# The wo load moved two value places up in the stream of a decode attention kernel, and its products moved behind its landing

## The chip, the cores and the metric

The kernel runs on one core of one Trainium2 chip. The metric is the device time of one execution in microseconds (us), taken from runs without the profiler; shown is the median of three. One more execution was taken with the profiler, and all views of the profile are of that one.

## The reference

One token is decoded. A gate mixes an attention block over a long key and value cache with a small gated MLP:

```python
def _A_ref(x, k_cache, v_cache, wq, wo):      # H = 32 heads, 65536 cached rows, Dh = 128, D = 512
    q = (x @ wq).reshape(B, Sq, H, Dh).transpose(0, 2, 1, 3)
    scores = jnp.einsum("bhqd,bhkd->bhqk", q, k_cache) * (Dh ** -0.5)
    p = _softmax(scores, axis=-1)
    o = jnp.einsum("bhqk,bhkd->bhqd", p, v_cache)
    return o.transpose(0, 2, 1, 3).reshape(B, Sq, H * Dh) @ wo
...
g = _sigmoid((x * gate_w).sum(-1, keepdims=True))
b = (silu(x @ w_gate) * (x @ w_up)) @ w_down  # F = 1792
return g * a + (1 - g) * b
```

All arrays are bf16. The keys and values of each head are 16 MiB each, so the two caches hold 1 GiB. The weight wo is 4096 x 512, 4 MiB.

## The kernel before, in words

**The stream.** Keys and values come through a ring of four slots of 4 MiB (`ring`, `NPL = 4`). A slot's filling is called a place: a quarter of one head's keys or of its values, 128 partitions by 128 cache rows. `plan_stream` writes the order of the places by hand: first wq, the MLP's weights and the keys of heads 0 and 1; then, for head h from 2 to 31, key places of head h alternating with value places of head h - 2; at last the eight value places of heads 30 and 31. The list `dmas` follows that order, and SyncE (SP) issues its entries one after another (L172 to L191). Ahead of each entry SP waits until the slot's former owner is used up: a key place by VectorE's transposes (`ktdone`), a value place by TensorE's products (`pvdone`). All waits and issues are on one queue, so an entry that waits holds back all that follow. The last value place of head 31 is issued in four parts that end at rows 64, 96, 112 and 128 (`ENDS`).

**wo.** It doesn't go through the ring. It is written into `kt`, the buffer of the transposed keys, which is free once the last scores have been computed; SP therefore waits for `qkdone` at `UN * H` (L187) before it issues wo. In `dmas` it stands behind the last value place of head 30, written ("v", H - 2, PL - 1) (L84). It has 32 x 128 rows of 1 KB; a place has 128 rows of 32 KB.

**Keys.** VectorE transposes half a place at a time (a unit, L334) from the ring to `kt`, and TensorE multiplies 16 times per unit into `psS` (L406). After a head's eight units come the maximum, the exponential on ScalarE and a transpose to `pb`.

**Values.** `values(h, t)` (L416) takes one place: 32 products of four cache rows each into row tile `psO` (L427), behind a wait for the landing. In place 1 of each head `turn` (L437) follows for the head before: eight small products that turn its finished row (`orow`, which ScalarE copied from `psO`) to a column in `psT`; ScalarE copies it to `oTn` (L234). The last place of all, ("v", H - 1, PL - 1), has another form: ahead of it `turn(H - 1)` brings what places 0 to 2 of head 31 gave to `psT` (ScalarE's copy for it is L262), and then 128 small products, row by row, are added there (L432).

**The output projection.** `project(h)` (L445) is one TensorE product of head h's column `oTn` with its 128 rows of wo, 1 x 512, added up in `psY` over all heads. It waits for ScalarE's copy of that column (`s_oc`), for the last head for VectorE's (`s_otn`). Behind `project(H - 1)` VectorE mixes in the MLP's row (L353), and ScalarE's queue stores the result.

**TensorE's order** at the end is the loop over `last` (L473 to L483): the places of heads 30 and 31 in turn; behind place 0 of head 31 a wait for wo's landing and `project` of heads 0 to 29; behind its place 1 (and the turn of head 30) `project` of head 30; then place 2, the turn of head 31, place 3 and `project` of head 31.

In the profile's lines an issue by SP is `SPq ... L191`, a value place is `psO ... L427 x32`, a product with wo is `psY ... L450`, a turn is `psT ... L441`, and the last place `psT ... L432 x128`.

## Time and profile before

| what | before |
|---|---|
| median of three runs | 2542.88 us (2542.84 to 2543.08) |
| profiled execution | 2542.47 us |
| its span, first to last instruction | 2540.6 us |
| mean granted TensorE clock | 0.914 |
| TensorE busy | 2046.1 us (81%) |
| VectorE busy | 1169.2 us (46%) |
| ScalarE busy | 56.8 us (2%) |
| key places on SP's queue | 128 of 4096 KB, 30.0 us from issue to landing (median) |
| whole value places on SP's queue | 127 of 4096 KB, 28.0 us (median) |
| wq, the first transfer of all | 4096 KB, 13.1 us |

The span is what the profile shows, and 1.87 us of the profiled execution's time lie around it. Busy shares are means over the whole span. The time from an issue to its landing holds the time that the transfers ahead of it on the queue still took. The chain of waits is followed back from the last instruction: at each step to what released it, or to the instruction before it on the same engine. An idle time in brackets at the end of a row is that of the engine just ahead of it, with what ended it.

### The profile page before, as it was taken

How to read it: one execution, taken by the hardware profiler on the slowest of the kernel's cores; microseconds unless marked ns; L12 is line 12 of the kernel's file. 1: busy time of each engine (PE TensorE's matmuls, PEld its weight loads, DVE VectorE, ACT ScalarE, POOL GpSimd, SP SyncE). 2: the span in 40 equal slices, each digit the busy share in tenths (PEclk: the TensorE clock that was granted, in tenths of full speed). 3: DMA queues.
4: the chain of work that ended last, by engine and by line, in shares of the span. 5: the costliest groups of instructions: out<-in, count | busy, mean ns of one | idle time of the engine just before them, and what ended most of it. 6: DMA issues, size and time to landing. Idle time of an engine off the chain costs nothing. (4 is left out here: it accounts for less than half of the span.)

```text
span 2540.6 us, 19360 instructions
## 1 busy us (share of the span) xinstructions
PE 2046.1 (81%) x8734; PEld 819.6 (32%) x8846; DVE 1169.2 (46%) x374; ACT 56.8 (2%) x194; POOL 26.1 (1%) x75
## 2 busy tenths in 40 slices
PE   5787788788878887888888888888887888788886
PEld 3333333333333333333333333333333333333333
DVE  4844544454454445444544444445445444444420
ACT  0000000000000000000000000000000000000000
POOL 0000000000000000000000000000000000000000
PEclk9989988998899889989899889998899888998898
DMA  9999999999999999999999999999999999999997
GB/s 414 431 432 430 432 431 433 431 431 434 430 431 433 432 430 433 431 430 432 434 430 431 434 431 431 434 430 431 433 432 430 434 431 430 433 432 431 432 425 317
DMA packets 42012, 1087.93 MB, mean 428 GB/s; under 512 B 4227, under 2 KB 8326, under 8 KB 8582
## 3 DMA queue, kind: packets, MB, share of 16 engines
q1 hardware_dynamic: 41988, 1087.65, 99.7%
q8 instruction: 11, 0.18, 0.0%
q14 instruction: 11, 0.09, 0.0%
q10 hardware_dynamic: 2, 0.00, 0.0%
HBM read 1087.64 MB, written 0.00 MB: 428 GB/s over the span
## 5 line engine op out<-in xcount | busy, mean ns | idle before, releaser
L334 DVE STREAM_TRANSPOSE kt<-ring 128x4096 uint32<-128x4096 uint32 x256 | 1125.7, 4426 | 1246.6 <-DMA ring<-in_A_k_cache_dram 1246.2
L406 PE MATMUL psS<-kt,qw 128*128 128x512 bf16 x3984 | 1095.7, 438 | 455.6 <-DVE kt L334 455.0
L427 PE MATMUL psO<-ring,pb 128*4 128x512 bf16 x4064 | 902.2, 380 | 19.4 <-DMA ring<-in_A_v_cache_dram 19.4
L406 PEld LDWEIGHTS psS<-kt,qw 128*128 128x128 bf16 x4096 | 425.7, 107 | 1111.3 <-DVE kt L334 420.8
L427 PEld LDWEIGHTS psO<-ring,pb 128*4 128x4 bf16 x4064 | 344.5, 87 | 568.8 <-issue 73.9
L246 ACT ACTIVATE nbias<-amx 128x1 f32<-128x1 f32 x32 | 6.5, 203 | 2348.6 <-POOL amx L212 2348.6
L350 DVE TENSOR_SCALAR oTn<-psT,Li 128x1 bf16<-128x1 f32 x1 | 0.2, 220 | 85.9 <-PE psT L432 85.9
L441 PEld LDWEIGHTS psT<-unit,orow 4*128 4x128 f32 x264 | 31.8, 186 | 15.1 <-issue 13.9
L212 POOL PARTITION_ALL_REDUCE amx<-mxs x32 | 11.3, 353 | 2369.1 <-DVE mxs L313 2369.1
L441 PE MATMUL psT<-unit,orow 4*128 4x1 f32 x264 | 34.6, 248 | 0.7 <-ACT orow L262 0.7
L319 DVE STREAM_TRANSPOSE pb<-pa 128x512 bf16<-128x512 bf16 x32 | 21.5, 671 | 6.4 <-PE psO L427 6.4
L313 DVE TENSOR_REDUCE mxs<-psS 128x1 f32<-128x512 f32 x32 | 20.9, 653 | 3.9 <-PE psS L406 3.9
L250 ACT ACTIVATE pa<-psS,nbias 128x512 bf16<-128x512 f32 x32 | 22.0, 687 | 2.6
L230 ACT ACTIVATE orow<-psO,Li 4x512 f32<-4x512 f32 x31 | 20.9, 675 | 21.6 <-PE psO L427 21.6
L214 POOL PARTITION_ALL_REDUCE Lt<-rsum x32 | 12.3, 385 | 38.0 <-ACT pa L250 38.0
L362 PE MATMUL psM<-ones,xrow 1*128 1x1 bf16 x4 | 0.3, 172 | 14.0 <-DMA gwrow<-in_gate_w_dram 14.0
L450 PE MATMUL psY<-kt,oTn 128*1 128x512 bf16 x32 | 7.6, 385 | 0.7 <-DVE oTn L350 0.4
L224 ACT COPY qw<-qd 128x16 bf16<-128x16 bf16 x32 | 7.9, 250 | 6.7 <-DVE qd L295 6.7
L383 PEld LDWEIGHTS psM<-xTb,ring 128*128 128x128 bf16 x112 | 6.9, 160 | 0.2
L383 PE MATMUL psM<-xTb,ring 128*128 128x1 bf16 x112 | 6.8, 198 | 0.0
L280 DVE CUSTOM_DVE_ANT_0 orow<-xrow,gwrow 1x512 f32<-1x512 bf16 x1 | 0.8, 837 | 12.0 <-DMA gwrow<-in_gate_w_dram 12.0
L234 ACT CAST oTn<-psT 128x1 bf16<-128x1 f32 x31 | 5.0, 162 | 55.6 <-PE psT L441 55.6
(41 smaller groups left out, 42.6 us busy)
## 6 DMA issues: line engine op xcount, KB each, us to landing
ring<-in_A_k_cache_dram SPq DMA_DIRECT2D x128, 4096.0 KB, 30.0
ring<-in_A_v_cache_dram SPq DMA_DIRECT2D x127, 4096.0 KB, 28.0
ring<-in_A_wq_dram SPq DMA_DIRECT2D x1, 4096.0 KB, 13.1
kt<-in_A_wo_dram SPq DMA_DIRECT2D x1, 4096.0 KB, 40.0
ring<-in_A_v_cache_dram SPq DMA_DIRECT2D x1, 2048.0 KB, 38.3
ring<-in_B_w_gate_dram SPq DMA_DIRECT2D x1, 1792.0 KB, 26.3
ring<-in_B_w_up_dram SPq DMA_DIRECT2D x1, 1792.0 KB, 30.0
ring<-in_B_w_down_dram SPq DMA_DIRECT2D x1, 1792.0 KB, 33.8
```

Source lines behind the costliest of these rows:

```text
L212: nc.gpsimd.partition_all_reduce(amx[:, h:h + 1], mxs[:, h:h + 1], P, RMAX).then_inc(s_ar, 1)
L214: nc.gpsimd.partition_all_reduce(Lt[:, h:h + 1], rsum[:, h:h + 1], P, RADD).then_inc(s_L, 1)
L224: nc.scalar.copy(qcol[:, h % 2], qd[:, h, :, :]).then_inc(s_qw, STEP)
L230: nc.scalar.mul(orow[0:4, :], psO[0:4, h % 2, :], Li[0:4, h:h + 1]).then_inc(s_or, STEP)
L250: nc.scalar.activation(pa[:, h % 2, :], psS[:, h % 2, :], ACT.Exp, bias=nbias[:, h:h + 1], scale=SCALE, accum_out=rsum[:, h:h + 1]).then_i ...
L313: nc.vector.reduce_max(mxs[:, h:h + 1], psS[:, h % 2, :], AX_X).then_inc(s_mx, 1)
L319: nc.vector.transpose(pb[:, h % 2, :], pa[:, h % 2, :]).then_inc(s_pb, STEP)
L334: nc.vector.transpose(o, src).then_inc(ktdone, 1)
L383: done = nc.tensor.matmul(psM[:, o + j:o + j + 1], w[:, c, :, j], xTb[:, c:c + 1], start=(c == 0), stop=(c == Dc - 1))
L406: done = nc.tensor.matmul(psS[:, h % 2, :], qw[:, h % 2, je, at0:at0 + 128], ktb[i % 2][:, je // 2, k, :, je % 2], start=(u == 0 and k == ...
L427: done = nc.tensor.matmul(psO[0:4, h % 2, :], pbk[:, h % 2, k, rho:rho + 4], v[:, r * Dh:(r + 4) * Dh], start=(t == 0 and r == 0), stop=(t ...
L441: done = nc.tensor.matmul(psT[:, h % 2:h % 2 + 1], orow[0:4, i * Dh:(i + 1) * Dh], unit[0:4, i:i + 1], start=(i == 0), stop=(i == 3 and h ...
```

## The change

wo's entry in `dmas` moves from behind place 3 of head 30 to behind its place 1, ahead of places 2 and 3. On TensorE the wait for wo's landing stands behind place 1 of head 30 and the turn that follows it; there the products of heads 0 to 28 are made. The product of head 29 stands behind place 2 of head 30. The product of head 30 moves from behind place 1 of head 31 to behind its place 2, ahead of the turn of head 31. The wait for `qkdone` ahead of wo's issue goes with the entry. The number of instructions on every engine is the same, and the order on VectorE, ScalarE and GpSimd is too.

```diff
@@ -81,7 +81,7 @@
-        if item == ("v", H - 2, PL - 1):
+        if item == ("v", H - 2, 1):
             landed["wo"] = len(dmas)
             dmas.append((("wo",), 0, 0, None, None))
@@ -474,11 +474,13 @@
                 if item == ("v", H - 1, PL - 1):
                     turn(H - 1)
                 run(item)
-                if item == ("v", H - 1, 0):
+                if item == ("v", H - 2, 1):
                     arrived(pe, landed["wo"])
-                    for h in range(H - 2):
+                    for h in range(H - 3):
                         project(h)
-                if item == ("v", H - 1, 1):
+                if item == ("v", H - 2, 2):
+                    project(H - 3)
+                if item == ("v", H - 1, 2):
                     project(H - 2)
             project(H - 1)
```

## The prediction

> I write V(h,t) for place t of head h's values; the last two heads are 30 and 31. All times are microseconds of the profiled execution's span unless said otherwise.

> **What bounds the kernel now.** First the page's DMA lines.

> ```profile
> q1 hardware_dynamic: 41988, 1087.65, 99.7%
> HBM read 1087.64 MB, written 0.00 MB: 428 GB/s over the span
> ```

> The 16 DMA engines are taken for 99.7% of the span, so the length is set by bytes. The change moves no byte in or out; it can only gain or lose where the last bytes have landed and work still follows, or by letting the queue run dry. So I read the end next, in the chain of waits over the last 45 us.

> ```profile
> 2457.57 43.09 DMA ring<-in_A_v_cache_dram
> ...
> 2500.80 9.41 PE psO L427 x32
> 2510.21 6.47 PE psY L450 x30
> 2516.68 6.91 PE psO L427 x32
> ...
> 2525.25 6.92 PE psO L427 x32
> ...
> 2533.92 3.35 PE psT L432 x128
> ```

> The reader is to see a DMA first, then an unbroken row of TensorE work: V(31,0), the 30 products with wo, V(31,1), V(31,2), V(31,3). From 2500.66 on, nothing waits for a landing. Is TensorE late against the stream there? The issues on SyncE's queue and their times to landing, read in narrow windows, answer it (timeline row: start, duration; issue row: size, us to landing).

> ```profile
> 2450.96 0.43 SPq L191 DMA_DIRECT2D kt<-in_A_wo_dram  x1
> kt<-in_A_wo_dram SPq DMA_DIRECT2D x1, 4096.0 KB, 40.0
> 2457.57 28.02 SPq L191 DMA_DIRECT2D ring<-in_A_v_cache_dram  x1
> ring<-in_A_v_cache_dram SPq DMA_DIRECT2D x1, 4096.0 KB, 43.1
> 2486.12 0.43 SPq L191 DMA_DIRECT2D ring<-in_A_v_cache_dram  x1
> ring<-in_A_v_cache_dram SPq DMA_DIRECT2D x1, 4096.0 KB, 34.0
> ```

> Start plus time to landing: wo at 2490.96, V(31,0) at 2500.67, V(31,2) at 2486.12 + 34.0 = 2520.1. The chain starts V(31,2) at 2525.25: TensorE is 5.1 late. V(31,3)'s last piece lands at 2488.16 + 41.8 = 2530.0, and its products run to 2533.92 + 3.35 = 2537.27. The lag was made at V(31,0): landed at 2500.66, it took 9.41, and the 30 products another 6.47, while the next place landed 9.7 later.

> Two other places are rows I need for prices, and three windows give TensorE's busy time and, after POOL's column, its granted clock.

> ```profile
> 2460.10 8.76 PE L427 MATMUL psO<-ring,pb 128*4 128x512 bf16 x32 [2.55 <-DMA ring<-in_A_v_cache_dram]
> ...
> 2479.61 7.07 PE L427 MATMUL psO<-ring,pb 128*4 128x512 bf16 x32 [2.73 <-DMA ring<-in_A_v_cache_dram]
> ```

> ```profile
> 2457.80:2461.20 3.40, 1.10 (x6) 0.46 (x7) 0.00 (x0) 0.00 (x0) 0.00 (x0) 1.00 1.01 434
> 2461.20:2464.60 3.40, 3.40 (x10) 1.03 (x9) 0.00 (x0) 0.00 (x0) 0.00 (x0) 0.50 0.96 410
> 2478.30:2481.70 3.40, 2.09 (x10) 0.88 (x11) 0.00 (x0) 0.00 (x0) 0.00 (x0) 1.00 1.09 344
> ```

> V(30,1) waited 2.55 and took 8.76, with half the clock granted over 3.4 us; V(30,3) waited 2.73 and took 7.07 at the full clock. The same place of work costs 1.69 more with the clock halved.

> **The change part by part.** *The DMA.* wo is issued behind V(30,1), ahead of V(30,2). SyncE's wait there, for all scores (L187), ends when the last score group does, at 2443.5; the slot wait of V(30,2), queued behind it, was over at 2439.74 (its issue row before), so this place is issued later. That costs nothing while the queue has work: V(30,0) lands at 2420.31 + 30.0 = 2450.3 and V(30,1) at 2432.05 + 28.0 = 2460.05, so 16.6 of cover. Behind wo the next issue is held, as V(31,0) was, for 28.02. It was let go at 2457.57 + 28.02 = 2485.59, which is 5.37 before wo's landing; I read the hold as wo's own packets, 4096 of 1 KB against 128 for a place, filling the queue. On that reading it ends again 5.37 before wo's landing, and the held place lands 9.7 behind wo, as V(31,0) did (2500.66 − 2490.96). V(30,3)'s and V(31,0)'s slots are free by then (V(29,3) done at 2450.5, V(30,0) at 2457.5), so the queue refills at once. wo needs 11.4 of the stream (2490.96 less V(30,3)'s landing, 2450.59 + 29.0 = 2479.6) wherever it stands.

> New landings: wo 2460.05 + 11.4 = 2471.4; V(30,2) 2481.2; V(30,3) 2490.9; V(31,0) 2500.7. From there all is as before: V(31,1) 2510.4, V(31,2) 2520.1, the last piece 2530.0. V(31,2)'s issue now waits for V(30,2)'s products, about 2488, and V(31,3)'s for V(30,3)'s, about 2498 to 2500; with landings due at 2520.1 and, for the first piece, 2525.0, that is 32 and 25 of notice, and the shortest 4 MB transfer of the page (wq, first in an empty queue) took 13.1. Moved past nothing on POOL's or ACT's queue; they issue no load.

> *The 29 products.* TensorE finishes V(30,1) and the turn of head 29 at 2469.8 (2468.79 + 1.05) and then waits for wo until 2471.4. Queued behind that wait are V(30,2), not landed before 2481.2, and through its products V(31,2)'s slot, with the notice above. 30 products took 6.47, so 29 take 6.3, to 2477.7; with the clock halved throughout twice that, to 2484.0. In the first case 3.5 of idle time are left, in the second V(30,2) starts 2.8 late and V(30,3), landing 9.7 later for 7.07 of work, is back on its landing. So these products cost nothing; their cover is the stream's landings, and without it they cost the 6.3 they cost now. The product of head 29 (0.22) falls into the wait before V(30,3).

> *The tail.* The 6.47 leave V(31,0)'s neighbourhood. Even at 9.41 V(31,0) is done at 2510.2, before V(31,1) lands at 2510.4; V(31,1) and the turn of head 30 take 7.07 + 1.05, to 2518.5 (or 2520.2), so V(31,2) starts on its landing, 2520.16, and ends 6.92 later at 2527.08. The product of head 30 (0.38 before, with its wait) now stands between V(31,2) and the last turn, within the 0.71 that ACT's copy of psO takes (2532.17 to 2532.88): free, and 0.4 at most if it were not. From V(31,2)'s end to the last product of V(31,3) it was 2537.28 − 2532.17 = 5.11, so now 2532.19. The last piece of V(31,3) lands at 2530.0 and is needed for the last 16 of 128 small products, at 2531.8: not binding. Gain, clock at full: 2537.28 − 2532.19 = 5.1. What follows (the last product, the mix, the store) is unchanged.

> *The unknown: the clock under V(31,2).* TensorE now idles before each place, which it did not there. The two rows above bound the loss: nothing (V(30,3)) or 1.69 (V(30,1)). They are equally near, since the idle time is alike and only its position against the 3.4 us stretches of the clock differs; I take half, 0.85. Gain 5.1 − 0.85 = 4.25.

> [...]

> *Sum.* The profiled execution took 2542.47 (span 2540.6 and 1.87 around it); 2542.47 − 4.25 = 2538.22. The median of the runs shown is 0.41 above the profiled one, so 2538.6.

> **The rivals.** (1) *A gap at wo.* For it: the held issue, with only 5.37 of the stream left when it was let go. If the hold is a length of 28 and not a state of the queue, V(30,2) is let go at 2443.9 + 28.0 = 2471.9, after wo has landed; by wq's row it lands 13.1 later, at 2485.0 and not 2481.2. All later landings move by 3.8, and the gain is 5.1 − 3.8 = 1.3: 2541.6. Against it: V(31,0) landed 9.7 behind wo, with no gap.

> (2) *Slower: the same hold, longer.* If SyncE is held 40.0, the time that wo took from issue to landing, V(30,2) is issued at 2483.9 and lands at 2497.0, 15.8 late: 2542.88 − 5.1 + 15.8 = 2553.6. The sign turns once the hold passes 28.0 + 1.3 = 29.3. Against it: the hold before ended ahead of wo's landing, and wo now has two places ahead of it and not three.

> (3) *wo lands late, the products stay in the way.* If wo needs its 40.0 from issue, it lands at 2483.9; the products end at 2490.2, V(30,2) at 2497.3, V(30,3) 2504.3, V(31,0) 2511.4, V(31,1) and its turn 2519.5, before 2520.1. Still 2537.8 to 2539.5: it changes nothing, but the notice for V(31,3)'s first piece falls to 21, above 13.1.

> **How the numbers follow.** The forecast, 0.84: the lag goes and V(31,2)'s landing sets the end, 2537.8 with the clock at full and 2539.5 without; 2538.6 between. Rival (1) 0.10, rival (2) 0.06; (3) is inside the forecast. A difference under 0.2%, 5.1 here, is about what a measurement of this kernel can't tell from no change, and the full-clock end lies just on that bound: of the 0.84 I put 0.30 beyond it. So faster 0.30, within 0.64, slower 0.06. The range: 2537.2 (full clock, and the 0.4 by which two executions may differ, in its favour, plus rounding) to 2540.4 (half clock, 0.9 towards rival (1)).

> **What would show it.** V(31,1) and V(31,2) each start within 0.2 of their landings, at about 2510.4 and 2520.2, with idle time before them ended by the ring's DMA; the chain runs through V(31,2) with no group of 30 products in it; the products stand near 2471.6 to 2478; SyncE's long hold sits on V(30,2), from 2443.9 to about 2466; the granted clock at 2520 to 2523 says which end of the range. Wrong it would be if V(30,2) landed over 10 behind wo, if V(31,2)'s landing moved off 2520.1, or if TensorE were still busy with V(31,1) when V(31,2) lands.

## The result, and the profile after

The changed kernel takes 2537.93 us, the median of 20 runs (2537.42 to 2539.44), against 2542.78 for the kernel before on the same chip (20 runs, 2541.44 to 2543.66). The ratio is 0.9983, 95% interval 0.9976 to 0.9990: a gain of 4.85 us, or 0.19%. The profiled execution took 2538.00 us with a span of 2536.1.

The chain of waits of the changed kernel, over the last 45 us (start, duration, what):

```profile
2488.91 31.71 DMA ring<-in_A_v_cache_dram
...
2520.66 7.09 PE psO L427 x32
...
2529.50 3.30 PE psT L432 x128
```

Before, this chain showed V(31,0), the 30 products, V(31,1) and V(31,2) in one row without a wait. Now it holds one place, V(31,2), which starts 0.04 us behind its landing. The group of 30 products is gone from it. The last product of V(31,3) ends at 2532.80; it was 2537.28.

The matmul timeline of the changed kernel shows where the products went and that every place now waits for its landing (start, duration; in brackets the idle time before and what ended it):

```profile
2472.09 7.88 PE L450 MATMUL psY<-kt,oTn 128*1 128x512 bf16 x29 [1.87 <-DMA kt<-in_A_wo_dram]
2481.80 7.07 PE L427 MATMUL psO<-ring,pb 128*4 128x512 bf16 x32 [1.84 <-DMA ring<-in_A_v_cache_dram]
...
2510.95 7.07 PE L427 MATMUL psO<-ring,pb 128*4 128x512 bf16 x32 [2.56 <-DMA ring<-in_A_v_cache_dram]
...
2520.66 7.07 PE L427 MATMUL psO<-ring,pb 128*4 128x512 bf16 x32 [1.66 <-DMA ring<-in_A_v_cache_dram]
```

The 29 products end at 2479.97, and V(30,2) still waits 1.84 us behind them. The issues on SyncE's queue (timeline row, then issue row with size and us to landing):

```profile
2443.95 0.39 SPq L191 DMA_DIRECT2D kt<-in_A_wo_dram  x1
kt<-in_A_wo_dram SPq DMA_DIRECT2D x1, 4096.0 KB, 28.1
2444.38 21.86 SPq L191 DMA_DIRECT2D ring<-in_A_v_cache_dram  x1
ring<-in_A_v_cache_dram SPq DMA_DIRECT2D x1, 4096.0 KB, 37.4
```

wo lands at 2443.95 + 28.1 = 2472.05. The issue behind it, now V(30,2), is held for 21.86 us, to 2466.24, which is 5.8 ahead of wo's landing, and V(30,2) lands at 2444.38 + 37.4 = 2481.8, 9.7 behind wo: the stream has no gap.

### The profile page after: what moved, and what is told of

Read it like the earlier page. It is cut to its first block, busy times and chain, and to the rows that moved or that the text cites. A ratio compares the mean times of both kernels' runs of the same rounds, so it can differ in the third digit from the quotient of the medians.

```text
span 2536.1 us, 19472 instructions
## 1 busy us (share of the span) xinstructions
PE 2080.9 (82%) x8846; PEld 819.7 (32%) x8846; DVE 1169.0 (46%) x374; ACT 56.7 (2%) x194; POOL 25.8 (1%) x75
## 3 DMA queue, kind: packets, MB, share of 16 engines
q1 hardware_dynamic: 41988, 1087.65, 99.9%
HBM read 1087.64 MB, written 0.00 MB: 429 GB/s over the span
## 4 chain that ended last, share of the span: by engine, by line
DMA 77%; DVE 11%; issue 11%; PE 1%; SPq 0%; ACT 0%; DVEq 0%; ACTq 0%
DMA ring<-in_A_k_cache_dram 74%; DVE kt L334 11%; DMA ring<-in_A_v_cache_dram 3%; PE psO L427 1%; PE psS L406 0%; PE psT L432 0%; PE psT L441 0%; SPq L191 0%; DVE fin L353 0%; PE psY L450 0%; ACT orow L262 0%; SPq L193 0%; SPq L194 0%; DVE oTn L350 0%; DVEq L349 0%
## 5 line engine op out<-in xcount | busy, mean ns | idle before, releaser
L406 PE MATMUL psS<-kt,qw 128*128 128x512 bf16 x4096 | 1129.5, 439 | 422.9 <-DVE kt L334 422.9
L427 PE MATMUL psO<-ring,pb 128*4 128x512 bf16 x4064 | 901.5, 380 | 12.1 <-DMA ring<-in_A_v_cache_dram 12.1
L427 PEld LDWEIGHTS psO<-ring,pb 128*4 128x4 bf16 x4064 | 344.2, 87 | 561.6 <-issue 60.1
L441 PEld LDWEIGHTS psT<-unit,orow 4*128 4x128 f32 x264 | 31.8, 186 | 14.9 <-issue 13.9
L450 PE MATMUL psY<-kt,oTn 128*1 128x512 bf16 x32 | 9.2, 440 | 2.3 <-DMA kt<-in_A_wo_dram 1.9
L250 ACT ACTIVATION_READ_ACCUMULATOR pa<-psS,nbias 128x1 f32 x32 | 6.2, 193 | 0.0
## 6 DMA issues: line engine op xcount, KB each, us to landing
ring<-in_A_k_cache_dram SPq DMA_DIRECT2D x128, 4096.0 KB, 30.0
ring<-in_A_v_cache_dram SPq DMA_DIRECT2D x127, 4096.0 KB, 28.0
ring<-in_A_wq_dram SPq DMA_DIRECT2D x1, 4096.0 KB, 13.1
kt<-in_A_wo_dram SPq DMA_DIRECT2D x1, 4096.0 KB, 28.1
```

Source lines behind the costliest of these rows:

```text
L250: nc.scalar.activation(pa[:, h % 2, :], psS[:, h % 2, :], ACT.Exp, bias=nbias[:, h:h + 1], scale=SCALE, accum_out=rsum[:, h:h + 1]).then_i ...
L406: done = nc.tensor.matmul(psS[:, h % 2, :], qw[:, h % 2, je, at0:at0 + 128], ktb[i % 2][:, je // 2, k, :, je % 2], start=(u == 0 and k == ...
L427: done = nc.tensor.matmul(psO[0:4, h % 2, :], pbk[:, h % 2, k, rho:rho + 4], v[:, r * Dh:(r + 4) * Dh], start=(t == 0 and r == 0), stop=(t ...
L441: done = nc.tensor.matmul(psT[:, h % 2:h % 2 + 1], orow[0:4, i * Dh:(i + 1) * Dh], unit[0:4, i:i + 1], start=(i == 0), stop=(i == 3 and h ...
L450: done = nc.tensor.matmul(psY[0:1, :], oTn[:, h:h + 1], wo_ap[:, h, :], start=(h == 0), stop=(h == H - 1))
```

## The experiments

Each kernel was timed beside the kernel before on the same chip; unless it says otherwise, an edit is against the changed kernel. Medians of the kernel before were 2542.27 to 2542.63 us in these comparisons. Times below are medians, with the lowest and highest run in brackets.

**The DMA alone.** wo's DMA two places up, the products where they were before:

```diff
-                if item == ("v", H - 2, 1):
+                if item == ("v", H - 1, 0):
                     arrived(pe, landed["wo"])
-                    for h in range(H - 3):
+                    for h in range(H - 2):
                         project(h)
-                if item == ("v", H - 2, 2):
-                    project(H - 3)
-                if item == ("v", H - 1, 2):
+                if item == ("v", H - 1, 1):
                     project(H - 2)
```

> wo's DMA stands two places up as in the changed kernel, the products stay behind V(31,0) as in the kernel before. Theory (the products' place made the lag): V(31,0) starts on its landing after a short idle and takes 7.07 to 8.76 us in place of 9.41, then 30 products 6.47; V(31,1), the turn and the product of head 30 follow, and V(31,2) starts 2.6 to 4.3 us behind its landing: 2540.5 to 2542.2 us. Rival (the earlier landing of wo itself brings the gain): 2537.9.

Measured: 2541.57 (2540.04 to 2543.07, 11 runs), ratio 0.9995 (0.9986 to 1.0004). The matmul timeline of the profiled execution (2542.35):

```profile
2501.49 8.75 PE L427 MATMUL psO<-ring,pb 128*4 128x512 bf16 x32 [2.74 <-DMA ring<-in_A_v_cache_dram]
2510.08 6.64 PE L450 MATMUL psY<-kt,oTn 128*1 128x512 bf16 x30
2516.56 7.07 PE L427 MATMUL psO<-ring,pb 128*4 128x512 bf16 x32
```

The row without brackets between V(31,0) and V(31,1) is back: the products stand there and nothing covers them. Landing wo early is worth 0.9 us by the medians by itself, and the interval doesn't keep that apart from nothing. The runs lie in two groups, 5 at 2540.04 to 2540.57 and 6 at 2541.57 to 2543.07; the expectation's 7.07 to 8.76 us for V(31,0) would give such a split, but only an execution of the upper group was profiled.

**The products alone.** wo's DMA where it was before (behind V(30,3)), the 30 products moved up by one place:

```diff
-        if item == ("v", H - 2, 1):
+        if item == ("v", H - 2, PL - 1):
             landed["wo"] = len(dmas)
...
-                if item == ("v", H - 2, 1):
+                if item == ("v", H - 2, PL - 1):
                     arrived(pe, landed["wo"])
-                    for h in range(H - 3):
+                    for h in range(H - 2):
                         project(h)
-                if item == ("v", H - 2, 2):
-                    project(H - 3)
```

> wo's DMA stays behind V(30,3) as in the kernel before; the 30 products go one place up, behind V(30,3), and the product of head 30 behind V(31,2). Theory: wo lands at about 2491, the products take 6.5 to 13 us by the clock and end between 2497.5 and 2504, at most 3.3 us behind V(31,0)'s landing, which is made up by V(31,2): 2537.9 us, as the changed kernel, spread 2537.4 to 2539.5. Rival (the DMA must move for the gain): 2541 to 2543.

Measured: 2538.21 (2537.27 to 2540.08, 11 runs), ratio 0.9984 (0.9975 to 0.9993). Nearly the whole gain, 4.2 us by the medians, comes without moving the DMA. Before, TensorE stood idle for 14.1 us ahead of V(31,0), and wo had landed 9.7 us before the end of that idle time; it only had to be used there. In the matmul timeline of this kernel:

```profile
2492.07 8.32 PE L450 MATMUL psY<-kt,oTn 128*1 128x512 bf16 x30 [4.19 <-DMA kt<-in_A_wo_dram]
2501.88 7.07 PE L427 MATMUL psO<-ring,pb 128*4 128x512 bf16 x32 [1.48 <-DMA ring<-in_A_v_cache_dram]
```

**The clock's part of the old lag.** The kernel before, with 60 additional products of constants (`sel` with itself, into the unused bank of `psQ`) in that idle time, used nowhere:

```diff
+            def keep(n):
+                for _ in range(n):
+                    nc.tensor.matmul(psQ[0:4].rearrange("p a b -> p (a b)"), sel[:, 0, 0:4],
+                                     sel[:].rearrange("p a b -> p (a b)"), start=True, stop=True)
...
+                if item == ("v", H - 2, 3):
+                    keep(60)
```

> The kernel before with 60 additional products of constants into an unused PSUM bank between V(30,3) and V(31,0), where TensorE waited 14 us for wo and V(31,0); their result is used nowhere. Theory: the lag of 5.1 us has a part of the clock: V(31,0) takes 7.07 in place of 9.41, so 2542.8 - 2.3 = 2540.4 us. Rival (the lag is the products' 6.47 alone): 2542.8, or slower if the additional products hold V(31,0) up.

Measured: 2540.21 (2539.85 to 2540.66, 11 runs), ratio 0.9991 (0.9982 to 1.0000). V(31,0) and V(31,2) in its matmul timeline:

```profile
2500.72 7.07 PE L427 MATMUL psO<-ring,pb 128*4 128x512 bf16 x32 [1.24 <-DMA ring<-in_A_v_cache_dram]
...
2522.67 7.07 PE L427 MATMUL psO<-ring,pb 128*4 128x512 bf16 x32
```

V(31,0) takes 7.07 in place of 9.41 (before, the granted clock was 0.50 from 2491.92 to 2505.56), and V(31,2) starts 2.66 behind its landing at 2520.01. In the same view it stood at 2525.09 before, 4.97 behind (the chain of waits, by which the prediction reads 5.1, puts the start at 2525.25). So 2.3 us of the lag were the clock after the long wait, and the other 2.7 the products, less the slack of the places after them.

**The same amount of work, twice, at both places.** In the changed kernel 29 additional products of constants behind the 29; in the kernel before, 30 behind its 30:

```diff
                     for h in range(H - 3):
                         project(h)
+                    keep(H - 3)
```

> The changed kernel with 29 additional products of constants into an unused PSUM bank right behind the 29 with wo; their result is used nowhere. Theory (the place is covered by landings): they push V(30,2) 1 to 4 us behind its landing, which is made up by V(31,0): 2537.9 us. Rival (the cover is used up by the 29, with the clock partly halved): part of 6.3 us reaches the end, 2539 to 2544.

> The kernel before with 30 additional products of constants into an unused PSUM bank right behind its 30 with wo; their result is used nowhere. Theory (nothing covers that place): all of 30 x 0.216 = 6.5 us reach the end, 2542.6 + 6.5 = 2549.1 us. Rival (the lag is made elsewhere): less than 3 us.

Measured: 2537.71 (2537.47 to 2538.62, 10 runs) at the new place, 2548.78 (2548.21 to 2549.70, 10 runs) at the old one; ratios to the kernel before 0.9981 (0.9972 to 0.9990) and 1.0024 (1.0015 to 1.0033). At the new place 6.4 us more of work cost nothing, at the old one 30 x 0.216 = 6.5 us cost 6.2. The profile of the first shows the cover being used and refilled: V(30,2) starts 5.3 late, and two places on nothing is late any more.

```profile
2480.22 6.42 PE L457 MATMUL psQ<-sel 128*4 128x512 bf16 x29
2486.48 7.07 PE L427 MATMUL psO<-ring,pb 128*4 128x512 bf16 x32
...
2493.60 14.24 PE L427 MATMUL psO<-ring,pb 128*4 128x512 bf16 x64
2510.39 8.76 PE L427 MATMUL psO<-ring,pb 128*4 128x512 bf16 x32 [2.55 <-DMA ring<-in_A_v_cache_dram]
```

V(30,2) has a row without brackets, V(30,3) and V(31,0) run as one, and V(31,1) waits 2.55 for its landing again. My expectation had put V(30,2) 1 to 4 us late.

**What holds SyncE.** wo's DMA in two halves, behind V(30,1) and behind V(30,2), and all 30 products behind V(30,2):

```diff
-        if item == ("v", H - 2, 1):
+        if item in (("v", H - 2, 1), ("v", H - 2, 2)):
             landed["wo"] = len(dmas)
-            dmas.append((("wo",), 0, 0, None, None))
+            dmas.append((("wo",), (item[2] - 1) * H // 2, 0, None, None))
...
-                    dst, src = wo_ap, wo_dram
+                    dst, src = wo_ap[:, r0:r0 + H // 2, :], wo_dram[:, r0:r0 + H // 2, :]
...
-                if item == ("v", H - 2, 1):
+                if item == ("v", H - 2, 2):
                     arrived(pe, landed["wo"])
-                    for h in range(H - 3):
+                    arrived(pe, landed["wo"] - 2)
+                    for h in range(H - 2):
                         project(h)
-                if item == ("v", H - 2, 2):
-                    project(H - 3)
```

> The changed kernel with wo's DMA in two halves of 16 heads' rows, one behind V(30,1) and one behind V(30,2), and all 30 products behind V(30,2). Theory (SyncE's hold is a state of the queue and follows the wo rows still to be moved): the issue behind each half is let go 5 to 7 us before that half lands, so V(30,2)'s at about 2459 to 2461 and V(30,3)'s at about 2475 to 2477, not 22 or 28 us after it began. Rival (the hold has a length of its own): 22 to 28 us each, and the second half is issued only at 2466 or later. Time about that of the changed kernel.

Measured in one profiled execution: 2538.77. The queue's timeline and issue rows:

```profile
2445.46 0.39 SPq L191 DMA_DIRECT2D kt<-in_A_wo_dram  x1
kt<-in_A_wo_dram SPq DMA_DIRECT2D x1, 2048.0 KB, 20.0
2445.89 13.88 SPq L191 DMA_DIRECT2D ring<-in_A_v_cache_dram  x1
2459.81 0.43 SPq L191 DMA_DIRECT2D kt<-in_A_wo_dram  x1
kt<-in_A_wo_dram SPq DMA_DIRECT2D x1, 2048.0 KB, 21.3
2460.29 15.04 SPq L191 DMA_DIRECT2D ring<-in_A_v_cache_dram  x1
```

The first half lands at 2465.46 and the issue behind it was let go at 2445.89 + 13.88 = 2459.77, 5.7 earlier; the second lands at 2481.1, let go at 2475.33, 5.8 earlier. With the whole load it was 5.4 (before) and 5.8 (after). Holds of 28.0, 21.9, 13.9 and 15.0 us thus end at the same distance from wo's landing: the hold followed what of wo was still to be moved and had no length of its own. Rows and bytes were halved together here. That it is the 1 KB rows and not the bytes is argued from the other issues: V(31,2)'s in the changed kernel, behind a whole place of as many bytes that was still on its way, took 0.33 us.

**The clock under V(31,2).** The 20 runs of the changed kernel fall into two groups: 11 from 2537.42 to 2538.00, and 9 from 2538.44 to 2539.44. First, additional products fill the waits ahead of the last places:

```diff
+                if item == ("v", H - 2, 2):
+                    keep(7)
+                if item == ("v", H - 2, 3):
+                    keep(10)
+                if item == ("v", H - 1, 0):
+                    keep(10)
+                if item == ("v", H - 1, 1):
+                    keep(6)
```

> The changed kernel with 7, 10, 10 and 6 additional products of constants into an unused PSUM bank behind V(30,2), V(30,3), V(31,0) and V(31,1) with its turn, where TensorE idles 1.7 to 2.7 us before each landing. Theory (the spread of 2537.4 to 2539.4 between executions is the clock under V(31,2)): all executions at 2537.4 to 2538.0, median 2537.5. Rival (the spread has another cause): the same spread; or slower by up to 1.5 if the additional products delay a place.

Measured: 2537.91 (2537.39 to 2538.74, 11 runs). One run in 11 lies above 2538.2, where 9 of 20 had; the median is not the 2537.5 that I expected, and a spread of 1.3 us stays. The spans on record tell what stays. Without the filling the two groups have spans of 2535.5 to 2536.1 and 2536.5 to 2537.6; with it all 11 have 2535.6 to 2536.2. The run of 2538.74 has a span of 2536.1 and 2.6 us around it, where the 20 runs of the changed kernel have 1.7 to 1.9. So the filling removes the upper group, and the rest of the spread lies mostly outside the span, from a cause that is open. To see the upper group itself, the changed kernel was profiled twice more, unchanged.

> The changed kernel once more, to find an execution of its upper group. If the clock under V(31,2) makes the groups, an execution above 2538.4 shows half the clock granted for some of V(31,2) and 7.4 to 8.8 us for its products, and one below 2538.1 shows 7.07. Rival: an upper one with V(31,2) at 7.07 and all landings about 1 us later.

> As the run before it: the changed kernel unchanged, for an execution of its upper group, with the same two readings.

Measured: 2537.58 and 2539.14, one of each group. V(31,1) and V(31,2) in the first, then in the second (matmul timeline):

```profile
2510.53 8.51 PE L427 MATMUL psO<-ring,pb 128*4 128x512 bf16 x32 [2.56 <-DMA ring<-in_A_v_cache_dram]
...
2520.24 7.07 PE L427 MATMUL psO<-ring,pb 128*4 128x512 bf16 x32 [0.21 <-DMA ring<-in_A_v_cache_dram]
```

```profile
2510.68 7.07 PE L427 MATMUL psO<-ring,pb 128*4 128x512 bf16 x32 [1.07 <-DMA ring<-in_A_v_cache_dram]
...
2520.40 8.76 PE L427 MATMUL psO<-ring,pb 128*4 128x512 bf16 x32 [1.67 <-DMA ring<-in_A_v_cache_dram]
```

V(31,2) landed at 2520.20 and 2520.35, nearly alike. In the execution of 2537.58 the slow place was V(31,1) (clock of 0.50 from 2510.08 to 2513.49), whose extra 1.44 us fell into the wait for V(31,2) and cost nothing; in that of 2539.14 it was V(31,2), with nothing behind it to absorb 1.69. The later landing and the clock make 1.84 us, the two executions differ by 1.56: what follows V(31,2) won back some 0.3. The grant in windows of the second (TensorE's busy time first, the clock behind POOL's column):

```profile
2517.73:2521.14 3.41, 1.74 (x13) 1.27 (x13) 0.00 (x0) 0.16 (x1) 0.00 (x0) 1.00 0.98 416
2521.15:2524.55 3.40, 3.40 (x10) 1.05 (x8) 0.00 (x0) 0.00 (x0) 0.00 (x0) 0.50 0.99 410
```

Half the clock, for 3.4 us, right under V(31,2), as the expectation of these two executions had it; its rival, landings 1 us later with V(31,2) at 7.07, did not occur.

**Earlier starts for the last places.** What sets the end now is V(31,2), worked on only when it has landed whole. So it, and then V(31,1) too, is issued in the four parts that V(31,3) has:

```diff
-            if item == ("v", H - 1, PL - 1):
+            if item[0] == "v" and item[1] == H - 1 and item[2] >= PL - 2:
                 parts = [(a, b) for a, b in zip((0,) + ENDS, ENDS)]
```

> The changed kernel with V(31,2) issued in the four parts that V(31,3) has (rows 64, 32, 16, 16). Theory (V(31,2)'s whole landing at 2520.6 sets the end): V(31,2) starts behind the turn of head 30, at 2519.0, and ends about 1.6 us earlier: 2536.3 us. Rival (the last landing sets the end already, or the smaller packets cost as much as they bring): 2537.9 or more.

> The changed kernel with V(31,1) and V(31,2) both issued in four parts. Theory: TensorE is through V(31,2) some 4 us earlier and the last part of V(31,3), landed at 2530.5, sets the end; its 16 products end at about 2531.0 in place of 2532.8: 2536.1 us, and the clock under V(31,2) no longer counts, so all executions lie within 2535.6 to 2537.0. Rival (the three extra issues and smaller packets delay the stream): the last landing moves by 0.2 to 1 us, 2536.3 to 2537.1.

(The second has `PL - 3`.) Measured: 2536.29 (2535.93 to 2537.81, 10 runs), ratio to the kernel before 0.9977 (0.9968 to 0.9987), and 2536.32 (2535.64 to 2537.46, 9 runs), ratio 0.9976 (0.9967 to 0.9986). Both beat the changed kernel by about 1.6 us, by medians taken on different occasions. With two split, the chain of waits goes through the last landing:

```profile
2505.61 24.98 DMA ring<-in_A_v_cache_dram
2530.59 0.05 issue
2530.64 0.60 PE psT L432 x16
```

That is what was expected, but its runs still spread over 1.8 us, where I had expected 1.4 and no clock under V(31,2) that counts. The spread lies in the spans (2533.9 to 2535.7); one profile doesn't tell from what. Last, the single split with the waits filled ahead of V(30,3), V(31,0) and V(31,1) (`keep` of 7, 10 and 10):

> The changed kernel with V(31,2) issued in four parts, and 7, 10 and 10 additional products of constants into an unused PSUM bank behind V(30,2), V(30,3) and V(31,0). Theory (with V(31,2) split, V(31,1)'s clock makes the upper executions): median 2536.0 us, none above 2537.0, where the split alone went up to 2537.8. Rival (the spread comes from the landings): the same spread, 2535.9 to 2537.8.

Measured: 2536.17 (2535.79 to 2536.84, 11 runs), ratio to the kernel before 0.9976 (0.9967 to 0.9985). The upper runs (3 of 10 at 2537.47 to 2537.81 without the filling) are gone; the median hardly moves. The spans say the same, 2534.0 to 2534.8 in place of 2534.1 to 2536.0, but 3 in 10 are few, and no upper execution of the single split was profiled: that V(31,1)'s clock made them is argued, not shown.

## Why the prediction was right, point by point

**The bound and the lag: shown.** TensorE was late at the end, and the lag came from V(31,0) on the halved clock and from the products behind it. Taking away the one (2.2 us by the medians), leaving the other where it stood (the DMA alone, 2541.57) and doubling it (6.2 us) each moved the end about as worked out beforehand.

**The DMA part: shown.** wo landed at 2472.05 (2471.4 worked out), V(30,2) 9.7 later; V(31,2)'s issue came at 2488.91 (about 2488) and had 31.7 of notice (32). The reading of the hold as a state of the queue, chosen over a hold of 28 us, was the step on which rivals (1) and (2) hung: it ended at 2466.24 where "about 2466" stood, and the two halves showed the same distance. Both rivals fall. Rival (3) did not occur: wo needed 28.1 from its issue, not 40.

**The products at no cost: shown, and with more to spare than said.** They took 7.88, partly on the halved clock (0.50 from 2471.66 to 2475.07), within the 6.3 to 12.6 given, and twice the number still cost nothing.

**What the prediction did not see: the DMA need not move.** It priced the two edits together. The products alone, one place up, give 2538.21, 0.3 above the changed kernel and well within the intervals, so no gain of the DMA's move beside it was measured.

**The size.** In the profiled execution the end came 4.5 earlier, not the 5.1 of the open clock, since this execution's stream was 0.4 later already when V(30,0) landed (2450.7 against 2450.3), ahead of the change, and V(31,2) landed at 2520.62. For that reason the landing off 2520.1, which the prediction names as a sign of being wrong, doesn't speak against it; in the two other executions it was 2520.20 and 2520.35. The allowance for the clock, 0.85 as half of 1.69, stood for a cost that is either paid or not: 9 of 20 runs lie in the upper group. Half was thus a fair guess of how often, and the mean of the runs, 2538.23, is nearer the forecast of 2538.6 than the median of 2537.93. As a forecast of a median the term was mis-sized: a median falls into one group or the other, near 2537.8 or 2539.5 by the prediction's own sum. Which one was luck: with 11 runs to 9 it is the upper edge of the lower group, and two runs more in the upper group would have put it at 2538.4 or above.

**The clock behind a wait.** Behind waits of 1.67 to 2.74 us a place took 8.51 to 8.76 us in place of 7.07 in four executions shown above, and in the two of them whose clock is on record it was 0.50 over one stretch of 3.4 us. The length of the wait alone doesn't decide it, since behind 2.56 us V(31,1) took 7.07 in one execution and 8.51 in another; the last section shows what went with it.

## What to carry to other kernels

In a kernel bound by its stream, look at the end for the place from which an engine no longer waits for a landing: work put behind that point cost nearly its full time here (6.2 of 6.5 us), and the same work put ahead of landings that must be waited for anyway cost nothing, as far as the waits up to the end could make it up. Try the order of the compute alone before the order of the loads. A cost like that of the clock here, where 9 of 20 runs lie in the upper group, is either paid or not in each execution; say how often, since half of it is no run's time.

## What the runs showed of the hardware that was not expected

The small products of a turn did not keep the clock at full here. Two windows of the changed kernel, one with a turn and one with products of a place alone, each with the window behind it:

```profile
2468.24:2471.65 3.41, 1.98 (x13) 1.21 (x11) 0.00 (x0) 0.16 (x1) 0.00 (x0) 1.00 1.07 454
2471.66:2475.07 3.41, 2.98 (x8) 0.89 (x9) 0.00 (x0) 0.00 (x0) 0.00 (x0) 0.50 0.89 384
2509.21:2512.61 3.40, 1.66 (x8) 0.70 (x9) 0.00 (x0) 0.00 (x0) 0.00 (x0) 1.00 0.92 395
2512.62:2516.03 3.41, 3.41 (x18) 1.39 (x16) 0.00 (x0) 0.00 (x0) 0.00 (x0) 1.00 0.95 408
```

The cost under V(31,2), paid in some executions only, goes with the same measure. The wait before it was 1.66 us in the execution of 2538.00 and 1.67 in that of 2539.14, but the work fell differently on the windows. In the slow one the window at 2517.73, in which V(31,2) starts, held 1.74 us, 1.00 of them the turn. In the other the windows at 2516.03 and 2519.44 held 1.93 and 2.19 without the turn.

wo's load of 1 KB rows held the issue behind it on SyncE until 5.4 to 5.8 us before it landed, for 28.0 us before and 21.9 after. It cost nothing: the held place landed 9.7 us behind wo before and after, with no gap in the stream.
